# One decode step of attention with a gate: heads loaded whole into six slots, queries and gate made first, keys multiplied in place

## The chip, the cores and the metric

The kernel runs on one core of one Trainium2 chip. The core has a matrix engine (PE; its weight loads are shown apart as PEld), a vector engine (DVE), a scalar engine (ACT), GpSimd (POOL) and a queue engine (SP) that issues the loads; 16 transfer engines (DMA) carry them out. SBUF is the memory that the engines read, PSUM the one that PE writes. Lower is better: the metric is the device time in microseconds, the median of several runs. Instructions are named by their line in the kernel, as L204.

## The reference, cut to what matters

One token (`x`, 512 values) is normalised, attends to a cache of 8192 keys and values in each of 32 heads, and is multiplied by a gate. All is in float32.

```python
xn = layernorm(x)                                   # 512
q  = (xn @ wq).reshape(32, 128)                     # wq 512 x 4096
s  = einsum("hd,hkd->hk", q, k_cache) * 128**-0.5   # k_cache 32 x 8192 x 128
o  = einsum("hk,hkd->hd", softmax(s), v_cache)      # v_cache 32 x 8192 x 128
a  = o.reshape(4096) @ wo                           # wo 4096 x 512
g  = silu((sigmoid(xn @ w_gate) * (xn @ w_up)) @ w_down)   # 512 x 1376 twice, 1376 x 512
out = x + a * g
```

Keys and values are 268 MB, `wq` and `wo` 8.39 MB each, the gate's three weights 8.45 MB together. Each byte is used once.

## The kernel before

All loads go through SP's one queue, in the order in which the code asks for them, into ten slots of 16 KB per partition (`stream`). A load waits in the queue until its slot has no reader left. A head's 8192 cached rows lie as 64 rows on each of 128 partitions; a load brings 32 of the 64 (`CB`), so keys and values of a head are four loads of 2 MB. Head 0 and head 31 are cut smaller. Keys are asked for two heads ahead, values in the head itself. `wq` comes in four chunks of eight heads, `wo` in chunks of eight heads when these heads are done (the last ones in pieces), and the gate's weights in six pieces in heads 2 to 7.

The queries are needed on every partition. `queries(c)` (L130) makes them so at once: the normalised token is copied into 128 columns (`xnb`) and is the stationary operand, so that each partition of the result holds the same row `qb`.

For a head, DVE does the scores: `scores` (L199) takes 16 rows at a time, multiplies them by the query into a tile `prod` (L204; two buffers) and sums along the 128 values (L205), four times for a head. `row_max` (L207) takes the maximum on each partition and PE turns it into a row (`pt`, L211); `all_max` (L214) takes the maximum of that row on DVE (L215), PE spreads it (`pm`, L217), ACT scales it (L218) and makes the exponentials `pr` with their row sums `rs` (L221). `norm` (L230) adds the row sums over partitions on PE (`pl`, L232) and takes the reciprocal on DVE (`rl`, L234). `weighted` (L223) multiplies by the values: 64 matmuls of one column by 128, on four column tiles of PE that write partitions 0, 32, 64 and 96 (`po`, L226). A float32 matmul is two passes in the profile, so a head has 128 of them. `finish` (L236) turns the four partial rows into a column (`pT`, L240), and `project` (L244) multiplies it by `wo` into `acc` (L246).

The heads are a pipeline: in the pass for head h the scores of head h, the maximum of head h - 1 and the values of head h - 2 are written (`values(h - 2)`, L292). The order on each engine is then set by the framework's scheduler, which may move an instruction ahead of others. The gate is done in heads 9 and 11 (`glu_hidden` L165 with `pgu` L172 and `hid`, `glu_out` L179 with `pd` L185 and `g_row`).

Of the kernel before, what the change touches and what calls it, by code (L numbers as in the profile page):

```python
# [18 lines left out]
def kernel(  # L19
# [21 lines left out]
    FT = (F + P - 1) // P  # L41
    NG = 4                 # column tiles of the tensor engine
    GP = P // NG
    SCALE = float(Dh) ** -0.5
# [10 lines left out]
    slot_words = CB * Dh  # L55

    def slot(name, words):
        assert words <= slot_words
        return stream.tile([P, slot_words], F32, tag="stream", name=name)
# [3 lines left out]
    # rows of the output stand on the first partition of each column tile  # L63
    GC = D // NG
    x_row = const.tile([P, GC], F32, name="x_row")
    nc.vector.memset(x_row, 0.0)

    wq_t, wo_t, kv_t = {}, {}, {}

    def load_wq(c):  # L70
        t = slot(f"wq{c}", KT * HG * Dh).rearrange("p (k n) -> p k n", k=KT)
        nc.sync.dma_start(
            t, wq[:, c * HG * Dh:(c + 1) * HG * Dh].rearrange("(p k) n -> p k n", k=KT))
        wq_t[c] = t

    def load_rows(which, src, h, b0, n):
        t = slot(f"{which}{h}_{b0}", n * Dh)
        nc.sync.dma_start(
            t[:, :n * Dh],
            src[0, h, b0 * P:(b0 + n) * P, :].rearrange("(p j) d -> p (j d)", p=P))  # L80
        kv_t[which, h, b0] = t[:, :n * Dh].rearrange("p (j d) -> p j d", d=Dh)

    def load_wo(h0, n):
        t = slot(f"wo{h0}", n * D)[:, :n * D].rearrange("p (h e) -> p h e", e=D)
        nc.sync.dma_start(t, wo[h0 * Dh:(h0 + n) * Dh, :].rearrange("(h p) e -> p h e", p=Dh))
        for i in range(n):
            wo_t[h0 + i] = t[:, i, :]

    load_rows("k", k_cache, 0, 0, SB)
    nc.sync.dma_start(x_col, xv.rearrange("(p k) -> p k", k=KT))  # L90

# [7 lines left out]

    load_wq(0)  # L100
    for b in range(SB, NB, SB):
        load_rows("k", k_cache, 0, b, SB)
    nc.sync.dma_start(x_row[0:P:GP, :], xv.rearrange("(g c) -> g c", g=NG))

# [19 lines left out]
    xnb = const.tile([P, KT, P], F32, name="xnb")  # L124
    nc.vector.tensor_copy(xnb, xn.rearrange("p (k o) -> p k o", o=1).to_broadcast([P, KT, P]))

# [1 line left out]
    qb = const.tile([P, H * Dh], F32, name="qb")  # L128

    def queries(c):  # L130
        for n in range(HG * Dh // 512):
            pq = ps_big.tile([P, 512], F32, tag="ps_big", name=f"pq{c}_{n}")
            for k in range(KT):
                nc.tensor.matmul(pq, xnb[:, k, :], wq_t[c][:, k, n * 512:(n + 1) * 512],  # L134
                                 start=(k == 0), stop=(k == KT - 1))
            o0 = c * HG * Dh + n * 512
            nc.scalar.copy(qb[:, o0:o0 + 512], pq)  # L137

# [1 line left out]
    gl = {}  # L140

    def load_glu(step):
        hk = KT // 2
        if step < 4:
            name, src = (("wg", w_gate), ("wu", w_up))[step // 2]
            i = step % 2
            t = slot(f"{name}{i}", hk * F)[:, :hk * F].rearrange("p (k f) -> p k f", f=F)
            nc.sync.dma_start(t, src.rearrange("(p k) f -> p k f", k=KT)[:, i * hk:(i + 1) * hk, :])
            for k in range(hk):
                gl[name, i * hk + k] = t[:, k, :]  # L150
        else:
            f0, f1 = ((0, 6), (6, FT))[step - 4]
            t = slot(f"wd{f0}", (f1 - f0) * D)[:, :(f1 - f0) * D].rearrange("p (t e) -> p t e", e=D)
            full = min(f1, F // P)
            nc.sync.dma_start(t[:, :full - f0, :],
                              w_down[f0 * P:full * P, :].rearrange("(t p) e -> p t e", p=P))
            if full < f1:
                nc.sync.dma_start(t[:F - full * P, full - f0, :], w_down[full * P:F, :])
            for i in range(f0, f1):
                gl["wd", i] = t[:, i - f0, :]  # L160

    hid = const.tile([P, FT], F32, name="hid")
    g_row = const.tile([P, GC], F32, name="g_row")

    def glu_hidden():  # L165
        pgu = ps_big.tile([P, 512], F32, tag="ps_big", name="pgu")
        fl = F - (FT - 1) * P
        for a, name in enumerate(("wg", "wu")):
            for t in range(FT):
                m = min(P, F - t * P)  # L170
                for k in range(KT):
                    nc.tensor.matmul(pgu[:m, a * FT + t:a * FT + t + 1],  # L172
                                     gl[name, k][:, t * P:t * P + m], xn[:, k:k + 1],
                                     start=(k == 0), stop=(k == KT - 1))
        for rows, c0, c1 in ((P, 0, FT - 1), (fl, FT - 1, FT)):
            nc.scalar.activation(hid[:rows, c0:c1], pgu[:rows, c0:c1], AF.Sigmoid)  # L176
            nc.vector.tensor_mul(hid[:rows, c0:c1], hid[:rows, c0:c1], pgu[:rows, FT + c0:FT + c1])  # L177

    def glu_out():  # L179
        pd = ps_big.tile([P, 512], F32, tag="ps_big", name="pd")  # L180
        nc.vector.memset(pd[:, :GC], 0.0)
        for t in range(FT):
            m = min(P, F - t * P)
            for g in range(NG):
                nc.tensor.matmul(pd[g * GP:g * GP + 1, :GC], hid[:m, t:t + 1],  # L185
                                 gl["wd", t][:m, g * GC:(g + 1) * GC],
                                 start=(t == 0), stop=(t == FT - 1))
        nc.scalar.activation(g_row, pd[:, :GC], AF.Sigmoid)
        nc.vector.tensor_mul(g_row, g_row, pd[:, :GC])

# [6 lines left out]
    sc, mx, pr, rs, rl, oT = {}, {}, {}, {}, {}, {}  # L197

    def scores(h, b, n, i):  # L199
        if b + i == 0:  # L200
            sc[h] = work.tile([P, NB], F32, tag="sc", name=f"sc{h}")
        q = qb[:, h * Dh:(h + 1) * Dh].rearrange("p (o d) -> p o d", o=1).to_broadcast([P, n, Dh])
        prod = work.tile([P, SB, Dh], F32, tag="prod", name=f"prod{h}_{b + i}")
        nc.vector.tensor_mul(prod[:, :n, :], kv_t["k", h, b][:, i:i + n, :], q)  # L204
        nc.vector.reduce_sum(sc[h][:, b + i:b + i + n], prod[:, :n, :], axis=AX.X)  # L205
# [8 lines left out]
    def all_max(h, pt):  # L214
        nc.vector.reduce_max(mx[h][:1, 1:2], pt, axis=AX.X)  # L215
        pm = ps_s.tile([P, 1], F32, tag="ps_s", name=f"pm{h}")
        nc.tensor.matmul(pm, ones[:1, :], mx[h][:1, 1:2], start=True, stop=True)  # L217
        nc.scalar.mul(mx[h][:, 2:3], pm, -SCALE)  # L218
        pr[h] = work.tile([P, NB], F32, tag="pr", name=f"pr{h}", bufs=3)
        rs[h] = work.tile([P, 1], F32, tag="rs", name=f"rs{h}", bufs=3)  # L220
        nc.scalar.activation(pr[h], sc[h], AF.Exp, bias=mx[h][:, 2:3], scale=SCALE, accum_out=rs[h])  # L221

    def weighted(h, b0, n):  # L223
        for j in range(n):
            g = (b0 + j) % NG
            nc.tensor.matmul(po[h % 2][g * GP:g * GP + 1, :], pr[h][:, b0 + j:b0 + j + 1],  # L226
                             kv_t["v", h, b0][:, j, :],
                             start=(b0 + j < NG), stop=(b0 + j >= NB - NG))

    def norm(h):  # L230
        pl = ps_s.tile([P, 1], F32, tag="ps_s", name=f"pl{h}")
        nc.tensor.matmul(pl, ones, rs[h], start=True, stop=True)  # L232
        rl[h] = work.tile([P, 1], F32, tag="rl", name=f"rl{h}", bufs=3)
        nc.vector.reciprocal(rl[h], pl)  # L234

    def finish(h):  # L236
        o1 = work.tile([P, Dh], F32, tag="o1", name=f"o1_{h}")
        nc.scalar.copy(o1, po[h % 2])  # L238
        pT = ps_s.tile([P, 1], F32, tag="ps_s", name=f"pT{h}")
        nc.tensor.matmul(pT, o1, rl[h], start=True, stop=True)  # L240
        oT[h] = work.tile([P, 1], F32, tag="oT", name=f"oT{h}", bufs=HG + 2)
        nc.scalar.copy(oT[h], pT)

    def project(h):  # L244
        for g in range(NG):
# [106 lines left out]
```

## Time and profile before

| | |
|---|---|
| runs, median (lowest to highest) | 709.97 us (709.45 to 710.28), 3 runs |
| profiled execution, first to last instruction | 707.6 us |
| DVE busy | 586.9 us, 83% |
| PE busy / weight loads | 326.5 us, 46% / 223.7 us, 32% |
| ACT busy | 46.4 us, 7% |
| read from HBM | 293.67 MB, 415 GB/s over the span |
| transfer engines in use by SP's queue | 98.9% |
| granted TensorE clock, mean | 0.657 of full speed |

The profiled execution has no time of its own beside its span; the span is 2.4 us below the median of the runs. In a timeline's row stand the start (us), the time taken (us), engine, line and operation, the tiles (written<-read) with their shapes, how many instructions are merged in the row (x2), and in brackets how long the engine was idle before and what ended that. In a table of waits stand the engine and line that waited, what it waited for, and the sum in us, the times and the longest. In a table of windows stand the stretch, its length, busy time of PE, PEld, DVE, ACT and POOL, each with its count, the granted clock, the share of the transfer engines and GB/s.

### The profile page before, as it was taken

To read this page: it belongs to the slowest core of one execution; us is meant where nothing else is said; L and a number is where in the kernel's file an instruction comes from. 1 tells how busy PE (TensorE), PEld (TensorE's weight loads), DVE (VectorE), ACT (ScalarE), POOL (GpSimd) and SP (SyncE) were. 2 spreads that over 40 slices of the span, in tenths; PEclk is the share of its full clock that TensorE was granted. 3 is DMA by queue.
4 is the path that set the end of the run, shared out by engine and by line. 5 is a ranking of instruction groups with operands and counts; after the bars stand their busy time and mean duration, and the time that the engine had idled before them with its cause. 6 is when DMAs were issued, how large, how long until landed. Compare 5 with 4: busy or idle time off the path is not lost.

```text
span 707.6 us, 10924 instructions
## 1 busy us (share of the span) xinstructions
PE 326.5 (46%) x4940; PEld 223.7 (32%) x4940; DVE 586.9 (83%) x374; ACT 46.4 (7%) x178; POOL 0.7 (0%) x6
## 2 busy tenths in 40 slices
PE   3231444449974323444572244444463353334466
PEld 1021332228863222333251132223132232222244
DVE  1999988886058799888888898888888998888970
ACT  0010000000101101000000000000010000000000
POOL 0000000000000000000000000000000000000000
PEclk9655676667566665555586666655576676665558
DMA  8999999999999999999999999999999999999995
GB/s 349 432 423 427 425 430 425 421 427 370 400 421 400 428 427 426 427 423 424 428 429 412 430 426 425 426 428 423 427 427 428 414 427 428 429 426 423 425 416 239
DMA packets 28413, 294.36 MB, mean 416 GB/s; under 512 B 2664, under 2 KB 2672, under 8 KB 10704
## 3 DMA queue, kind: packets, MB, share of 16 engines
q1 hardware_dynamic: 28368, 293.68, 98.9%
q8 instruction: 38, 0.62, 0.4%
q14 instruction: 7, 0.06, 0.0%
HBM read 293.67 MB, written 0.00 MB: 415 GB/s over the span
## 4 chain that ended last, share of the span: by engine, by line
DVE 64%; issue 17%; PE 16%; DMA 3%; ACT 0%; SPq 0%
DVE prod L204 33%; DVE sc L205 28%; PE pgu L172 4%; PE pt L211 2%; PE pm L217 2%; PE pq L134 2%; PE pl L232 2%; PE po L226 2%; DMA wq<-in_A_wq_dram 1%; DMA wo<-in_A_wo_dram 1%; DVE mx L215 1%; DVE mx L209 1%; DVE rl L234 1%; PE pd L185 0%; ACT qb L137 0%
## 5 line engine op out<-in xcount | busy, mean ns | idle before, releaser
L204 DVE TENSOR_TENSOR prod<-k,qb 128x2048 f32<-128x2048 f32 x129 | 287.0, 2264 | 9.7 <-ACT qb L137 9.7
L205 DVE TENSOR_REDUCE sc<-prod 128x16 f32<-128x2048 f32 x129 | 286.5, 2261 | 0.0
L226 PE MATMUL po<-v,pr 128*1 128x128 f32 x4096 | 175.7, 347 | 52.2 <-DMA v<-in_A_v_cache_dram 50.2
L226 PEld LDWEIGHTS po<-v,pr 128*1 128x1 f32 x4096 | 121.1, 104 | 99.8 <-DMA v<-in_A_v_cache_dram 56.7
L211 PE MATMUL pt<-ident,mx 128*1 128x128 f32 x64 | 18.5, 391 | 274.8 <-DVE mx L209 274.8
L211 PEld LDWEIGHTS pt<-ident,mx 128*1 128x1 f32 x64 | 2.8, 81 | 278.4 <-DVE mx L209 258.4
L134 PE MATMUL pq<-wq,xnb 128*128 128x512 f32 x64 | 38.9, 775 | 3.8 <-DMA wq<-in_A_wq_dram 3.8
L234 DVE RECIPROCAL rl<-pl 128x1 f32<-128x1 f32 x32 | 5.3, 167 | 41.1 <-PE pl L232 41.1
L215 DVE TENSOR_REDUCE mx<-pt 1x1 f32<-1x128 f32 x32 | 8.9, 278 | 31.2 <-PE pt L211 31.2
L218 ACT ACTIVATE mx<-pm 128x1 f32<-128x1 f32 x32 | 5.5, 171 | 309.5 <-PE pm L217 309.5
L238 ACT COPY o<-po 128x128 f32<-128x128 f32 x32 | 8.5, 265 | 253.6 <-PE po L226 253.6
L217 PEld LDWEIGHTS pm<-mx,ones 1*128 1x128 f32 x64 | 15.7, 302 | 29.7 <-DVE mx L215 29.7
L217 PE MATMUL pm<-mx,ones 1*128 1x1 f32 x64 | 18.4, 354 | 14.0 <-DVE mx L215 13.9
L240 PE MATMUL pT<-rl,o 128*128 128x1 f32 x64 | 12.6, 266 | 25.5 <-DVE rl L234 14.6
L134 PEld LDWEIGHTS pq<-wq,xnb 128*128 128x128 f32 x64 | 15.9, 256 | 23.8 <-issue 23.8
L240 PEld LDWEIGHTS pT<-rl,o 128*128 128x128 f32 x64 | 9.9, 195 | 35.0 <-ACT o L238 20.1
L232 PE MATMUL pl<-rs,ones 128*128 128x1 f32 x64 | 18.4, 357 | 0.0
L172 PE MATMUL pgu<-xn,wu 128*128 128x1 f32 (+1 forms) x88 | 18.4, 345 | 0.0
L172 PEld LDWEIGHTS pgu<-xn,wu 128*128 128x128 f32 (+1 forms) x88 | 18.3, 325 | 0.0
L232 PEld LDWEIGHTS pl<-rs,ones 128*128 128x128 f32 x64 | 15.7, 306 | 0.7 <-issue 0.2
L177 DVE TENSOR_TENSOR hid<-hid,pgu 128x10 f32<-128x10 f32 (+1 forms) x2 | 0.3, 158 | 17.6 <-ACT hid L176 17.6
L172 PEld LDWEIGHTS pgu<-xn,wg 128*128 128x128 f32 (+1 forms) x88 | 13.5, 249 | 0.5 <-issue 0.5
(44 smaller groups left out, 91.8 us busy)
## 6 DMA issues: line engine op xcount, KB each, us to landing
k<-in_A_k_cache_dram SPq DMA_DIRECT2D x60, 2048.0 KB, 27.6
v<-in_A_v_cache_dram SPq DMA_DIRECT2D x60, 2048.0 KB, 25.8
wq<-in_A_wq_dram SPq DMA_DIRECT2D x4, 2048.0 KB, 21.9
k<-in_A_k_cache_dram SPq DMA_DIRECT2D x7, 1024.0 KB, 14.8
v<-in_A_v_cache_dram SPq DMA_DIRECT2D x7, 1024.0 KB, 23.4
wo<-in_A_wo_dram SPq DMA_DIRECT2D x3, 2048.0 KB, 22.8
wg<-in_B_w_gate_dram SPq DMA_DIRECT2D x2, 1376.0 KB, 26.8
wu<-in_B_w_up_dram SPq DMA_DIRECT2D x2, 1376.0 KB, 20.7
```

Of the source, the lines that this page charges most:

```text
L134: nc.tensor.matmul(pq, xnb[:, k, :], wq_t[c][:, k, n * 512:(n + 1) * 512], start=(k == 0), stop=(k == KT - 1))
L172: nc.tensor.matmul(pgu[:m, a * FT + t:a * FT + t + 1], gl[name, k][:, t * P:t * P + m], xn[:, k:k + 1], start=(k == 0), stop=(k == KT - 1))
L204: nc.vector.tensor_mul(prod[:, :n, :], kv_t["k", h, b][:, i:i + n, :], q)
L205: nc.vector.reduce_sum(sc[h][:, b + i:b + i + n], prod[:, :n, :], axis=AX.X)
L211: nc.tensor.matmul(pt, mx[h][:, 0:1], ident, start=True, stop=True)
L215: nc.vector.reduce_max(mx[h][:1, 1:2], pt, axis=AX.X)
L217: nc.tensor.matmul(pm, ones[:1, :], mx[h][:1, 1:2], start=True, stop=True)
L226: nc.tensor.matmul(po[h % 2][g * GP:g * GP + 1, :], pr[h][:, b0 + j:b0 + j + 1], kv_t["v", h, b0][:, j, :], start=(b0 + j < NG), stop=(b0 ...
L232: nc.tensor.matmul(pl, ones, rs[h], start=True, stop=True)
L234: nc.vector.reciprocal(rl[h], pl)
L238: nc.scalar.copy(o1, po[h % 2])
L240: nc.tensor.matmul(pT, o1, rl[h], start=True, stop=True)
```

## The change

Loads: ten slots of 16 KB become six of 32 KB per partition, and a load brings all 64 rows of a head's keys or values (4.19 MB). `wq` comes in two loads of half its rows, each gate weight in one load; they stand first in the queue, keys of head 0 behind them. `wo` comes last, in two halves (the second in three loads). Rows of `wo` and of `w_down` are dealt out to the partitions so that a partition's rows are neighbours in memory; for `w_down` this means that column t of a gate tile is every tenth column, and `wg` and `wu` are read with that step.

Queries: all 32 heads at once, as rows on partitions 0, 32, 64 and 96 (one column of `xn` is the stationary operand); `spread` (four heads at a time) multiplies such a row by ones to bring it to every partition. The gate follows at once. Scores: the product is written over the keys, and each product is followed by its own sum. Values: head h - 1 in the pass for head h, behind the first quarter of its scores, and `values` begins with `pl` and the reciprocal. The output columns are kept in `o_all`, and all projections follow the last head. `tc.manual_schedule()` keeps each engine's order as written.

```diff
-    CB = 32                # of those, rows in a load
-    HG = 8                 # heads in a chunk of wq or wo
+    SLOT = NB * Dh
+    ctx.enter_context(tc.manual_schedule())
-    stream = ctx.enter_context(tc.tile_pool(name="stream", bufs=10))
+    stream = ctx.enter_context(tc.tile_pool(name="stream", bufs=6))
...
+    nc.sync.dma_start(x_col, xv.rearrange("(p k) -> p k", k=KT))
+    load_wq(0)
+    nc.vector.memset(x_row, 0.0)
+    nc.sync.dma_start(x_row[0:P:GP, :], xv.rearrange("(g c) -> g c", g=NG))
+    load_wq(1)
+    load_gate("wg", w_gate)
+    load_gate("wu", w_up)
+    load_down()
...
+    for k in range(KT):
+        for b in range(NQ // NG):
+            for g in range(NG):
+                c = (b * NG + g) * QT
+                nc.tensor.matmul(pq[b][g * GP:g * GP + 1, :], xn[:, k:k + 1], wq_t[k][:, c:c + QT],
+                                 start=(k == 0), stop=(k == KT - 1))
+    for b in range(NQ // NG):
+        nc.scalar.copy(q_row[:, b, :], pq[b])
+    def spread(t):
+        b, g = divmod(t, NG)
+        pb = ps_big.tile([P, QT], F32, tag="ps_big", name=f"pb{t}")
+        nc.tensor.matmul(pb, ones[g * GP:g * GP + 1, :], q_row[g * GP:g * GP + 1, b, :],
+                         start=True, stop=True)
+        qb[t] = work.tile([P, QT], F32, tag="qb", name=f"qb{t}")
+        nc.scalar.copy(qb[t], pb)
+    spread(0)
...
+            cols = slice(t, FT * P, FT) if t < FT else slice(FT * P, F)
             for k in range(KT):
-                    nc.tensor.matmul(pgu[:m, a * FT + t:a * FT + t + 1],
-                                     gl[name, k][:, t * P:t * P + m], xn[:, k:k + 1],
+                nc.tensor.matmul(pgu[:m, a * NT + t:a * NT + t + 1], gl[name, k][:, cols], xn[:, k:k + 1],
                                  start=(k == 0), stop=(k == KT - 1))
...
-        prod = work.tile([P, SB, Dh], F32, tag="prod", name=f"prod{h}_{b + i}")
-        nc.vector.tensor_mul(prod[:, :n, :], kv_t["k", h, b][:, i:i + n, :], q)
-        nc.vector.reduce_sum(sc[h][:, b + i:b + i + n], prod[:, :n, :], axis=AX.X)
+        for j in range(j0, j1, SB):
+            kt = kv_t["k", h][:, j:j + SB, :]
+            nc.vector.tensor_mul(kt, kt, q)
+            nc.vector.reduce_sum(sc[h][:, j:j + SB], kt, axis=AX.X)
...
+        rows = slice(i * GP, (i + 1) * GP)
+        for r in range(R):
+            nc.tensor.matmul(pT[rows, r:r + 1], o1[:, r:Dh:R], rl[h], start=True, stop=True)
+        nc.scalar.copy(o_all[rows, w, :], pT[rows, :])
...
     for h in range(H):
-        for b, n in parts(h):
-            for i in range(0, n, SB):
-                scores(h, b, min(n, SB), i)
-                if b + i == 0 and h > 0:
-                    all_max(h - 1, pt)
-        if h > 1:
-            values(h - 2)
-        pt = row_max(h)
+        need(("k", h))
+        if h + 2 < H:
+            need(("k", h + 2))
+        if h % HT == HT - 2 and h + HT < H:
+            spread(h // HT + 1)
+        scores(h, 0, NB // 4)
+        if h > 0:
+            all_max(h - 1, pt)
+            need(("v", h - 1))
+            values(h - 1)
+        scores(h, NB // 4, NB)
+        pt = row_max(h)
+    need(order[-1])
+    all_max(H - 1, pt)
+    values(H - 1)
+    for w in range(NW):
+        project(w)
```

What this moves is seen in the rows of the engines' programs (line, operation, tile written<-tiles read; the number behind a name counts tiles). DVE, one head in the middle, before:

```order
L204 TENSOR_TENSOR prod_0_1475<-k_0_1174,qb 128x2048
L204 TENSOR_TENSOR prod_16_1485<-k_0_1174,qb 128x2048
L205 TENSOR_REDUCE sc_1474<-prod_0_1475 128x16
L205 TENSOR_REDUCE sc_1474<-prod_16_1485 128x16
L204 TENSOR_TENSOR prod_32_1488<-k_32_1176,qb 128x2048
L204 TENSOR_TENSOR prod_48_1491<-k_32_1176,qb 128x2048
L205 TENSOR_REDUCE sc_1474<-prod_32_1488 128x16
L205 TENSOR_REDUCE sc_1474<-prod_48_1491 128x16
L209 TENSOR_REDUCE mx_1568<-sc_1474 128x1
L215 TENSOR_REDUCE mx_1568<-pt_1570 1x1
L234 RECIPROCAL rl_1604<-pl_1602 128x1
```

DVE, one head in the middle, now (L213 is the product, L214 the sum, L218 the row maximum, L224 the maximum of the row `pt`, L236 the reciprocal):

```order
L213 TENSOR_TENSOR k_337<-k_337,qb_160 128x2048
L214 TENSOR_REDUCE sc_543<-k_337 128x16
L224 TENSOR_REDUCE mx_535<-pt_537 1x1
L236 RECIPROCAL rl_555<-pl_553 128x1
L213 TENSOR_TENSOR k_337<-k_337,qb_160 128x2048
L214 TENSOR_REDUCE sc_543<-k_337 128x16
L213 TENSOR_TENSOR k_337<-k_337,qb_160 128x2048
L214 TENSOR_REDUCE sc_543<-k_337 128x16
L213 TENSOR_TENSOR k_337<-k_337,qb_160 128x2048
L214 TENSOR_REDUCE sc_543<-k_337 128x16
L218 TENSOR_REDUCE mx_635<-sc_543 128x1
```

Products and sums alternate; the maximum of `pt` moved from the end of its own head into the next one, behind the first sum, and the reciprocal behind it now belongs to the same head as that maximum (before, to the head ahead of it).

DVE at the start, from the end of the normalisation to the first scores, before:

```order
L121 RECIPROCAL st<-st 128x1
L123 TENSOR_SCALAR xn<-xc,st 128x4
L125 COPY xnb<-xn 128x512
L204 TENSOR_TENSOR prod_0_156<-k_0_79,qb 128x2048
L204 TENSOR_TENSOR prod_16_159<-k_16_93,qb 128x2048
```

and now:

```order
L140 TENSOR_SCALAR xn<-xc,st 128x4
L147 MEMSET pq_120 128x512
L147 MEMSET pq_122 128x512
L184 TENSOR_TENSOR hid<-hid,pgu 128x10
L184 TENSOR_TENSOR hid<-hid,pgu 96x1
L186 MEMSET pd 128x128
L194 TENSOR_TENSOR g_row<-g_row,pd 128x128
L198 MEMSET acc 128x128
L201 MEMSET po_307 128x128
L201 MEMSET po_308 128x128
L213 TENSOR_TENSOR k_312<-k_312,qb_160 128x2048
```

The gate's two steps on DVE (`hid`, `g_row`) stand ahead of the first product. PE at the same place, before and then now:

```order
L134 MATMUL pq_0_127<-wq_91,xnb 128x512 x4
L134 MATMUL pq_1_133<-wq_91,xnb 128x512 x4
L211 MATMUL pt_170<-ident,mx_168 1x128
L217 MATMUL pm_185<-mx_168,ones 128x1
L226 MATMUL po_123<-v_0_147,pr_188 1x128 x16
```

```order
L153 MATMUL pq_122<-wq_85,xn 1x512 x4
L163 MATMUL pb_158<-q_row,ones 128x512
L180 MATMUL pgu<-xn,wg 128x1 x40
L180 MATMUL pgu<-xn,wg 96x1 x4
L180 MATMUL pgu<-xn,wu 128x1 x40
L180 MATMUL pgu<-xn,wu 96x1 x4
L190 MATMUL pd<-wd,hid 1x128 x44
L220 MATMUL pt_333<-ident,mx_331 1x128
L226 MATMUL pm_343<-mx_331,ones 128x1
L234 MATMUL pl_349<-rs_347,ones 128x1
L239 MATMUL po_307<-v_314,pr_346 1x128 x64
```

The gate's 88 and 44 matmuls moved from the tenth and twelfth head to the place between the queries and the first head's maximum, and `pl` of a head from two heads later to right behind its `pm`.

More of the change, by code (lines that the diff above doesn't have):

```diff
@@ L83, in load_wo, with load_wq @@
[L83 to L90, printed above, removed]
+    wq_t, kv_t, wo_t, gl = {}, {}, {}, {}
+    def load_wq(i):
+        n = KT // 2
+        t = slot(f"wq{i}").rearrange("p (k c) -> p k c", k=n)
+        nc.sync.dma_start(t, wq.rearrange("(p k) c -> p k c", k=KT)[:, i * n:(i + 1) * n, :])
+        for k in range(n):
+            wq_t[i * n + k] = t[:, k, :]
@@ new lines, in load_rows, with load_wo @@
+    def load_rows(which, src, h):
+        t = slot(f"{which}{h}")
+        nc.sync.dma_start(t, src[0, h].rearrange("(p j) d -> p (j d)", p=P))
+        kv_t[which, h] = t.rearrange("p (j d) -> p j d", d=Dh)
+    def load_wo(g0, n, cuts=()):
+        t = slot(f"wo{g0}").rearrange("p (g r e) -> p g r e", r=R, e=D)
+        src = wo[g0 * P * R:(g0 + n) * P * R, :].rearrange("(g p r) e -> p g r e", p=P, r=R)
+        m = n - 1 if cuts else n
+        nc.sync.dma_start(t[:, :m], src[:, :m])
+        for r0, r1 in cuts:
+            nc.sync.dma_start(t[:, m, r0:r1, :], src[:, m, r0:r1, :])
+        for i in range(n):
+            wo_t[g0 + i] = t[:, i]
@@ L123 @@
     nc.vector.tensor_scalar(xn, xc, st[:, 4:5], None, op0=ALU.mult)
[L124 to L132, printed above, removed]
+    q_row = const.tile([P, NQ // NG, QT], F32, name="q_row")
+    pq = []
+    for b in range(NQ // NG):
+        t = ps_big.tile([P, QT], F32, tag="ps_big", name=f"pq{b}")
+        nc.vector.memset(t, 0.0)
+        pq.append(t)
@@ L133, in queries @@
+    spread(0)
+    hid = const.tile([P, FT + 1], F32, name="hid")
+    g_row = const.tile([P, GC], F32, name="g_row")
+    pgu = ps_big.tile([P, 512], F32, tag="ps_big", name="pgu")
+    NT = FT + 1
+    for a, name in enumerate(("wg", "wu")):
+        for t in range(NT):
+            m = P if t < FT else FL
+            cols = slice(t, FT * P, FT) if t < FT else slice(FT * P, F)
             for k in range(KT):
-                nc.tensor.matmul(pq, xnb[:, k, :], wq_t[c][:, k, n * 512:(n + 1) * 512],
+                nc.tensor.matmul(pgu[:m, a * NT + t:a * NT + t + 1], gl[name, k][:, cols], xn[:, k:k + 1],
@@ L135, in queries @@
                                  start=(k == 0), stop=(k == KT - 1))
[L136 to L172, printed above, removed]
-                                     gl[name, k][:, t * P:t * P + m], xn[:, k:k + 1],
[L174 to L189, printed above, removed]
+    for rows, c0, c1 in ((P, 0, FT), (FL, FT, NT)):
+        nc.scalar.activation(hid[:rows, c0:c1], pgu[:rows, c0:c1], AF.Sigmoid)
+        nc.vector.tensor_mul(hid[:rows, c0:c1], hid[:rows, c0:c1], pgu[:rows, NT + c0:NT + c1])
@@ new lines @@
+    pd = ps_big.tile([P, 512], F32, tag="ps_big", name="pd")
+    nc.vector.memset(pd[:, :GC], 0.0)
+    for t in range(NT):
+        m = P if t < FT else FL
+        for g in range(NG):
+            nc.tensor.matmul(pd[g * GP:g * GP + 1, :GC], hid[:m, t:t + 1],
+                             gl["wd", t][:m, g * GC:(g + 1) * GC],
+                             start=(t == 0), stop=(t == NT - 1))
+    nc.scalar.activation(g_row, pd[:, :GC], AF.Sigmoid)
+    nc.vector.tensor_mul(g_row, g_row, pd[:, :GC])
@@ L218, in all_max @@
         nc.scalar.mul(mx[h][:, 2:3], pm, -SCALE)
-        pr[h] = work.tile([P, NB], F32, tag="pr", name=f"pr{h}", bufs=3)
-        rs[h] = work.tile([P, 1], F32, tag="rs", name=f"rs{h}", bufs=3)
+        pr[h] = work.tile([P, NB], F32, tag="pr", name=f"pr{h}")
+        rs[h] = work.tile([P, 1], F32, tag="rs", name=f"rs{h}")
         nc.scalar.activation(pr[h], sc[h], AF.Exp, bias=mx[h][:, 2:3], scale=SCALE, accum_out=rs[h])
[L223 to L228, printed above, removed]
@@ L230, in norm, with values @@
-    def norm(h):
+    def values(h):
         pl = ps_s.tile([P, 1], F32, tag="ps_s", name=f"pl{h}")
         nc.tensor.matmul(pl, ones, rs[h], start=True, stop=True)
-        rl[h] = work.tile([P, 1], F32, tag="rl", name=f"rl{h}", bufs=3)
+        rl[h] = work.tile([P, 1], F32, tag="rl", name=f"rl{h}")
         nc.vector.reciprocal(rl[h], pl)
-    def finish(h):
+        for j in range(NB):
+            g = j % NG
+            nc.tensor.matmul(po[h % 2][g * GP:g * GP + 1, :], pr[h][:, j:j + 1], kv_t["v", h][:, j, :],
+                             start=(j < NG), stop=(j >= NB - NG))
@@ L237, in finish @@
         o1 = work.tile([P, Dh], F32, tag="o1", name=f"o1_{h}")
         nc.scalar.copy(o1, po[h % 2])
[L239 to L245, printed above, removed]
-            nc.tensor.matmul(acc[g * GP:g * GP + 1, :], oT[h], wo_t[h][:, g * GC:(g + 1) * GC],
-                             start=(h == 0), stop=(h == H - 1))
@@ L270, with project @@
-    queries(0)
-    load_k(1)
+        w, i = divmod(h, R)
+        pT = ps_s.tile([P, R], F32, tag="ps_s", name=f"pT{h}")
+        rows = slice(i * GP, (i + 1) * GP)
+        for r in range(R):
+            nc.tensor.matmul(pT[rows, r:r + 1], o1[:, r:Dh:R], rl[h], start=True, stop=True)
+        nc.scalar.copy(o_all[rows, w, :], pT[rows, :])
+    def project(w):
+        for r in range(R):
+            for g in range(NG):
+                nc.tensor.matmul(acc[g * GP:g * GP + 1, :], o_all[:, w, r:r + 1],
+                                 wo_t[w][:, r, g * GC:(g + 1) * GC],
+                                 start=(w + r == 0), stop=(w == NW - 1 and r == R - 1))
@@ new lines, with issue, need @@
+    order = []
+    for h in range(H):
+        order.append(("k", h))
+        if h < H - 2:
+            order.append(("v", h))
+    order += [("v", H - 2), ("v", H - 1), ("wo", 0), ("wo", NW // 2)]
+    def issue(item):
+        which, i = item
+        if which == "wo":
+            load_wo(i, NW // 2, () if i == 0 else ((0, R - 1), (R - 1, R)))
+        else:
+            load_rows(which, k_cache if which == "k" else v_cache, i)
+    ahead = iter(order)
+    loaded = set()
+    def need(item):
+        while item not in loaded:
+            nxt = next(ahead)
+            issue(nxt)
+            loaded.add(nxt)
@@ L291 @@
-        if h > 1:
-            values(h - 2)
-        pt = row_max(h)
-        if (h + 2) % HG == 0 and h + 2 < H:
-            queries((h + 2) // HG)
-        if h == 9:
-            glu_hidden()
-        if h == 11:
-            glu_out()
-        if h > 2 and (h - 2) % HG == 0:
-            for i in range(h - 2 - HG, h - 2):
-                project(i)
-    for i in range(H - HG // 2, H):
-        load_wo(i, 1)
-    all_max(H - 1, pt)
-    values(H - 2)
-    for i in range(H - HG, H - HG // 2):
-        project(i)
@@ L311 @@
-    norm(H - 1)
-    for b, n in parts(H - 1):
-        weighted(H - 1, b, n)
-    for i in range(H - HG // 2, H - 2):
-        project(i)
-    finish(H - 1)
-    project(H - 2)
-    project(H - 1)
+            need(("k", h + 2))
[7 more added lines that the diff above has]
+        scores(h, NB // 4, NB)
+        pt = row_max(h)
```

80 lines of the change are left out of this document (29 added, 51 removed).

## The prediction

> **What bounds the kernel now.** I read the page's first and third parts, then the waits, then one head on the vector engine in order of time.
>
> ```profile
> span 707.6 us, 10924 instructions
> PE 326.5 (46%) x4940; PEld 223.7 (32%) x4940; DVE 586.9 (83%) x374; ACT 46.4 (7%) x178; POOL 0.7 (0%) x6
> q1 hardware_dynamic: 28368, 293.68, 98.9%
> ```
>
> Two resources are near full. The loads occupy the transfer engines for 98.9% of the span, and the vector engine (DVE) is busy for 83%. The waits tell which of them follows the other.
>
> ```profile
> SPq L78 <- DVE prod L204: 293.0, 48, 11.0
> DVE rl L234 <- PE pl L232: 41.1, 29, 8.1
> ```
>
> The load queue waits 293 us for DVE to free a slot. DVE never waits for keys; what it waits for is the small chain of the softmax (41.1 us for the sum behind `rl` alone). One head in the middle of the run:
>
> ```profile
> 303.69 0.22 DVE L209 TENSOR_REDUCE mx<-sc 128x1 f32<-128x64 f32 x1
> 304.58 0.28 DVE L215 TENSOR_REDUCE mx<-pt 1x1 f32<-1x128 f32 x1 [0.68 <-PE pt L211]
> 306.05 0.17 DVE L234 RECIPROCAL rl<-pl 128x1 f32<-128x1 f32 x1 [1.19 <-PE pl L232]
> 306.14 4.47 DVE L204 TENSOR_TENSOR prod<-k,qb 128x2048 f32<-128x2048 f32 x2
> 310.53 4.47 DVE L205 TENSOR_REDUCE sc<-prod 128x16 f32<-128x2048 f32 x2
> 314.92 4.49 DVE L204 TENSOR_TENSOR prod<-k,qb 128x2048 f32<-128x2048 f32 x2
> 319.31 4.47 DVE L205 TENSOR_REDUCE sc<-prod 128x16 f32<-128x2048 f32 x2
> 323.82 0.22 DVE L209 TENSOR_REDUCE mx<-sc 128x1 f32<-128x64 f32 x1
> ```
>
> From one row maximum to the next it is 20.13 us: four products and four sums, 17.6 us, and 2.5 us for the maximum, its two short waits and the reciprocal. A head's keys and values are 2 x 32768 x 128 bytes, 8.39 MB; at the 425 GB/s of a window below that is 19.7 us. So the two rates are nearly equal, DVE is a little the slower, and the load order lets the stream run ahead. Whatever lengthens DVE's head, or starts its first head later, therefore shows in the time almost in full.
>
> **The change, part by part.** First, the head on DVE. The products no longer go to two `prod` tiles, two products and then two sums, but in place: product, its own sum, next product. Two instructions that don't depend on each other start 2.20 us apart (306.14 to 310.53 for two), one alone lasts 4.47 - 2.20 = 2.27, and an instruction that reads its predecessor's result starts 0.04 after that one's end (319.31 + 4.47 to 323.82). A pair that depends costs 2.27 + 0.04 + 2.20 = 4.51 in place of 4.39. Four pairs: 18.04 us, 0.5 more than before. That the product overwrites its source I cost at nothing: the operand count and shape are as before. No row shows it; a row bound is 2.20 us for either kind of instruction, one element after the other, which leaves no gain.
>
> Second, the chain of a head's maximum, exponentials and sum. Before, the reciprocal behind head h - 1's maximum was that of head h - 2, whose row sums were long there; it waited only for the matrix engine (PE) to come round. Now it is head h - 1's own, so DVE stands still for the whole chain from the maximum to the sum. The links, in order of time, from the second last head:
>
> ```profile
> 667.13 0.28 DVE L215 TENSOR_REDUCE mx<-pt 1x1 f32<-1x128 f32 x1 [0.68 <-PE pt L211]
> 667.47 0.58 PE L217 MATMUL pm<-mx,ones 1*128 1x1 f32 x2 [0.37 <-DVE mx L215]
> 667.98 0.59 PE L232 MATMUL pl<-rs,ones 128*128 128x1 f32 x2
> 668.09 0.17 ACT L218 ACTIVATE mx<-pm 128x1 f32<-128x1 f32 x1 [4.73 <-PE pm L217]
> 668.29 0.35 ACT L221 ACTIVATE pr<-sc,mx 128x64 f32<-128x64 f32 x1
> 668.54 0.19 ACT L221 ACTIVATION_READ_ACCUMULATOR pr<-sc,mx 128x1 f32 x1
> ```
>
> From the maximum's end (667.41) to the row sums (668.73) it is 1.32 us; `pl` then needs 0.05 + 0.59 + 0.04. That is a wait of 2.00 us, where 1.19 stood. Against it, the wait of 0.68 for `pt` goes: a product and a sum, 4.5 us, now lie between the row maximum and its use. The head after the change is 18.04 + 0.28 + 2.00 + 0.09 (reciprocal, less the overlap with the next product) + 0.26 (last sum's end and row maximum) = 20.67 us, 0.54 more than before. Behind the waiting reciprocal stand the six large instructions left of the head; nothing else runs on DVE meanwhile. Head 0 has no such chain: 18.3. All heads: 18.3 + 31 x 20.67 = 659.1 us. The first exponentials also load their table, 1.28 us by a row below, now inside the wait: 1.3 once.
>
> Third, the start, where most of the time goes. Before, 1 MB of keys and 2 MB of `wq` came first and DVE began the first head at 19.06 us. Now all of `wq` (8.39 MB) and of the gate's weights (8.45 MB) stand ahead of the first keys, and the written order keeps the gate's last product ahead of the first head on DVE. Rates of the loads at the start, and what PE does for the queries and the copies after them:
>
> ```profile
> 2.00:14.00 12.00, 3.24 (x7) 2.07 (x8) 1.69 (x8) 0.28 (x2) 0.00 (x0) 1.00 0.98 376
> 14.00:20.00 6.00, 6.00 (x11) 2.45 (x11) 0.94 (x1) 0.58 (x1) 0.00 (x0) 1.00 1.04 440
> 20.00:40.00 20.00, 2.43 (x7) 0.65 (x5) 20.00 (x11) 0.58 (x1) 0.00 (x0) 0.61 1.00 425
> 153.32 9.20 PE L134 MATMUL pq<-wq,xnb 128*128 128x512 f32 x16
> 18.45 0.58 ACT L137 COPY qb<-pq 128x512 f32<-128x512 f32 x1 [10.03 <-PE pq L134]
> ```
>
> The last column is GB/s: 4.51 MB by 14 us, 7.15 by 20, then 425. `wq` is complete at 22.9 us, 23.3 with the issue of `x_col` ahead of it. By the same rate the gate's three weights are in at 29.9, 36.5 and 43.1, and the first keys at 53.1. The query matmuls stand on one row of each column tile, as those of `po` do. Their second half is 32 passes of 512 columns; `po`'s 128-column passes take 0.051 us (6.49 / 128, row in the tail) or 0.030 (1.93 / 64), so 6.5 or 3.9 us; I take the middle, 5.2, to 28.5. Two copies of 0.58 with their gaps, 1.2, to 29.7; the spread of the first query is two passes at 9.20 / 16, 1.2, to 30.9. Then PE does the gate:
>
> ```profile
> 162.36 13.41 PE L172 MATMUL pgu<-xn,wg 128*128 128x1 f32 x88
> 175.63 0.99 PE L172 MATMUL pgu<-xn,wu 128*128 128x1 f32 x4
> 184.59 17.42 PE L172 MATMUL pgu<-xn,wu 128*128 128x1 f32 x84
> 163.00:168.00 5.00, 5.00 (x46) 5.00 (x45) 5.00 (x3) 0.14 (x1) 0.00 (x0) 0.98 1.02 434
> 190.00:196.00 6.00, 6.00 (x30) 6.00 (x29) 0.00 (x0) 0.00 (x0) 0.00 (x0) 0.50 1.05 438
> 202.04 0.18 ACT L176 ACTIVATE hid<-pgu 128x10 f32<-128x10 f32 x1 [15.65 <-PE pgu L172]
> 202.66 0.15 DVE L177 TENSOR_TENSOR hid<-hid,pgu 96x1 f32<-96x1 f32 x1 [0.23 <-ACT hid L176]
> 242.82 2.09 PE L185 MATMUL pd<-wd,hid 128*1 128x128 f32 x35
> 243.07 1.28 ACT L188 ACT_TABLE_LOAD   x1
> 245.50 0.29 DVE L189 TENSOR_TENSOR g_row<-g_row,pd 128x128 f32<-128x128 f32 x1 [2.40 <-ACT g_row L188]
> ```
>
> The first 176 passes took 31.8 us before, 0.109 us each at a granted clock of 0.98 and 0.200 at 0.50 (46 in 5 us, 30 in 6). They were spread over other work's time; now they lie on the path: from 30.9 to 62.7. The bounds are 176 x 0.109 = 19.2 and 176 x 0.200 = 35.2; I keep 31.8, since queries run ahead of the gate in both kernels. The hidden row's sigmoid and product, 0.8 (202.04 to 202.81), to 63.5; its 88 passes at 2.09 / 35, 5.3, to 68.8; the last sigmoid, product and three memsets, 1.1, to 69.9. So DVE starts the first head at 69.9 us, 16.8 after its keys are there. In front of it nothing else hides this: DVE has no other work.
>
> One more price lies in the gate. `wg` and `wu` are now read by every tenth column (a step of 40 bytes), where 128 neighbours were read. No row has such a read; the bounds are no change and, by the nearest row, twice the 31.8 us if each weight costs as much as two. I take no change, as the slow passes at clock 0.50 leave 1.6 ns for each weight. [...]
>
> Fourth, the tail, with the rows of before:
>
> ```profile
> 687.61 6.49 PE L226 MATMUL po<-v,pr 128*1 128x128 f32 x128
> 694.49 0.38 PE L240 MATMUL pT<-rl,o 128*128 128x1 f32 x2
> 695.88 1.93 PE L226 MATMUL po<-v,pr 128*1 128x128 f32 x64
> 704.45 0.29 DVE L321 TENSOR_TENSOR res<-g_row,acc 128x128 f32<-128x128 f32 x1 [8.29 <-PE acc L246]
> 705.09 0.60 SPq L323 DMA_DIRECT2D out_dram<-res  x1
> ```
>
> After the last row maximum come `pt` and the maximum (0.96), the chain (2.0), 128 passes of `po` (6.4), the copy (0.4), four `pT` pairs (1.2; four rows of 0.38 are the upper bound), a copy (0.3), and then all 256 projection passes, which before ran in four groups beside the heads. At 0.030 they take 7.7 us, at 0.051 13.1; I take 7.7, as PE has been busy since `po`. The end from 704.40 on is 3.2. Sum: 22.1 us, as much as before (685.57 to 707.6), so the projections' move eats what the late `wo` loads cost.
>
> Fifth, the stream. Pieces of 32 KB per partition and six slots hold 25 MB. A key slot comes free at its head's end, so its next keys are asked for two heads, 41 us, ahead and need 9.9 us plus at most one load in front. The loads are hidden; if that cover goes, each late piece costs DVE its lateness. That `wo` stands last costs nothing: its slots come free two heads before the end.
>
> The sum: 69.9 + 659.1 + 1.3 + 22.1 = 752.4 us of span. The profiled execution of before has 707.6 and the median of the runs is 710.0; with the same 2.4 us around it, 755 us.
>
> **The rivals.** *Weights by columns read at half speed.* For it: the step of 40 bytes, untested here. Against it: the passes are slow already. The start goes to 101.7, the time to 787. *The gate at the full clock.* For it: the windows from 2 to 20 us grant 1.00, and the query passes just ahead keep PE busy. Against it: in the same situation before, the clock fell to 0.50 within 10 us. The gate then takes 19.2 and the time is 742. *Faster: the stream sets the pace.* If the wait of 2.00 us vanished, a head would take 18.7, less than the loads' 19.7, and the time would be what 293.68 MB at 425 GB/s need, 691 us, with 2 at the start, 10 behind the last piece and the 2.4 around: 705. For it: 98.9% in the queue's row. Against it: the written order puts the reciprocal before three quarters of the head, with its own chain. It decides only where the wait falls below some 0.5 us: (710 - 2.4 - 69.9 - 18.3 - 1.3 - 22.1) / 31 = 19.2 us a head. *The loads come late.* If the large pieces ran at 390 GB/s for want of requests, a head would need 21.5 us and the time would be about 780. Against it: from the second head on two loads are waiting.
>
> **How the numbers follow.** The likeliest, a late start and a head of 20.7, has 0.62, with its own range from 748 to 762. Half-speed weights 0.17, the full clock 0.13, late loads 0.04, the stream 0.03, and 0.01 that gains and losses cancel. 0.2% is about what a measurement of this kernel can tell from no change. Slower are all but the last two, 0.96; faster 0.03, same 0.01. The range from 742 to 788 takes in the second and third case.
>
> **What would show it.** In the profile after: the first product on DVE near 70 us, behind `g_row`; the reciprocal's wait at 2.0 us each, 62 us in all; none of `mx` for `pt`; head after head 20.7 us apart; the loads' share near 93% and some load waits ended by DVE; 256 passes of `acc` in one piece at the end. I am wrong if the first product comes before 60 or after 80 us, if the heads lie under 20 us apart, or if DVE waits for keys.

## The result, and the profile after

| | median (lowest to highest) | profiled span |
|---|---|---|
| before | 709.71 us (708.85 to 710.28), 4 runs | 707.6 us |
| changed | 760.44 us (759.25 to 760.72), 4 runs | 758.9 us |

The changed kernel takes 1.071 times as long (95% interval 1.070 to 1.073): 51 us slower. The forecast was 755, in a range from 742 to 788. One of the four runs of the first experiment below, the profiled one, fell in a slower state of the chip and took 737.2 us, so its time there is the median of the other three, 699.9 us (700.2 with all four), and its profile is not used.

First the parts of the page of the changed kernel that answer to those shown of before.

```profile
span 758.9 us, 11178 instructions
PE 334.6 (44%) x5148; PEld 232.9 (31%) x5148; DVE 596.6 (79%) x373; ACT 43.6 (6%) x177; POOL 0.7 (0%) x6
q1 hardware_dynamic: 11424, 293.68, 92.6%
```

The same 293.68 MB in fewer packets, but the transfer engines are now idle for 7% of the span. The waits say for whom, of DVE and of the load queue:

```profile
DVE rl L236 <- PE pl L234: 64.9, 32, 3.3
DVE hid L184 <- ACT hid L183: 62.7, 2, 62.4
SPq L92 <- PE po L239: 356.0, 29, 13.1
SPq L92 <- DVE mx L218: 240.2, 29, 19.0
```

The queue waits for slots that DVE (keys) and PE behind DVE (values) free; DVE waits for keys in no row. Its own two large waits are the reciprocal's, 64.9 us in 32 heads, and the one ahead of the first head. One head of the changed kernel on DVE:

```profile
406.12 0.22 DVE L218 TENSOR_REDUCE mx<-sc 128x1 f32<-128x64 f32 x1
406.26 2.28 DVE L213 TENSOR_TENSOR k<-k,qb 128x2048 f32<-128x2048 f32 x1
408.64 2.29 DVE L214 TENSOR_REDUCE sc<-k 128x16 f32<-128x2048 f32 x1
410.85 0.27 DVE L224 TENSOR_REDUCE mx<-pt 1x1 f32<-1x128 f32 x1
413.10 0.17 DVE L236 RECIPROCAL rl<-pl 128x1 f32<-128x1 f32 x1 [1.99 <-PE pl L234]
413.19 2.27 DVE L213 TENSOR_TENSOR k<-k,qb 128x2048 f32<-128x2048 f32 x1
415.50 2.29 DVE L214 TENSOR_REDUCE sc<-k 128x16 f32<-128x2048 f32 x1
417.70 2.28 DVE L213 TENSOR_TENSOR k<-k,qb 128x2048 f32<-128x2048 f32 x1
...
426.86 0.22 DVE L218 TENSOR_REDUCE mx<-sc 128x1 f32<-128x64 f32 x1
```

From row maximum to row maximum it is 20.74 us. The maximum of `pt` no longer waits; the reciprocal behind it waits 1.99. The product over the keys takes 2.28, as the product into `prod` did.

The start, from the timelines of PE and DVE and a table of windows:

```profile
29.98 19.47 PE L180 MATMUL pgu<-xn,wg 128*128 128x1 f32 x88 [0.34 <-DMA wg<-in_B_w_gate_dram]
49.31 19.46 PE L180 MATMUL pgu<-xn,wu 128*128 128x1 f32 x88
69.86 4.79 PE L190 MATMUL pd<-wd,hid 128*1 128x128 f32 x88 [1.09 <-ACT hid L183]
75.04 0.29 DVE L194 TENSOR_TENSOR g_row<-g_row,pd 128x128 f32<-128x128 f32 x1 [5.28 <-ACT g_row L193]
75.70 2.27 DVE L213 TENSOR_TENSOR k<-k,qb 128x2048 f32<-128x2048 f32 x1
40.00:50.00 10.00, 10.00 (x49) 10.00 (x48) 0.00 (x0) 0.00 (x0) 0.00 (x0) 0.50 1.05 430
```

PE works on the gate from 29.98 to 68.8 us without a gap, most of it at a granted clock of 0.50. Then come `hid`, `pd` and `g_row`, and only then, at 75.70, the first product. The end, with the last row maximum of before (line L209) ahead of it:

```profile
685.35 0.22 DVE L209 TENSOR_REDUCE mx<-sc 128x1 f32<-128x64 f32 x1
```

```profile
737.91 0.22 DVE L218 TENSOR_REDUCE mx<-sc 128x1 f32<-128x64 f32 x1
740.97 6.53 PE L239 MATMUL po<-v,pr 128*1 128x128 f32 x128
747.89 0.46 PE L247 MATMUL pT<-rl,o 128*32 128x1 f32 x5 [0.40 <-ACT o L242]
748.38 7.17 PE L253 MATMUL acc<-wo,o_all 128*1 128x128 f32 x250
755.58 0.29 DVE L302 TENSOR_TENSOR res<-g_row,acc 128x128 f32<-128x128 f32 x1 [14.33 <-PE acc L253]
```

So the 51.3 us between the two profiled spans divide as follows. Before, DVE's first product was at 19.06 us.

| stretch | before | changed | difference |
|---|---|---|---|
| start to the first product on DVE | 19.06 | 75.70 | +56.6 |
| first product to the end of the last row maximum | 666.5 | 662.4 | -4.1 |
| from there to the end | 22.0 | 20.8 | -1.2 |

The middle is shorter, though a head takes 0.6 us longer, because before it also held the gate. DVE stood still for it three times, in all 32 us: 12.2 for `pt`, which came behind the gate's first passes on PE (the other waits of that row are 0.68 each), 17.6 for `hid` and 2.4 for `g_row`:

```profile
DVE mx L215 <- PE pt L211: 31.2, 29, 12.2
DVE hid L177 <- ACT hid L176: 17.6, 2, 17.3
DVE g_row L189 <- ACT g_row L188: 2.4, 1, 2.4
```

In return, DVE did its first four heads without a wait, in 9 us less than four later ones.

### The profile page after: what moved, and what is told of

Read it like the earlier page. It is cut to its first block, busy times and chain, and to the rows that moved or that the text cites. A ratio compares the mean times of both kernels' runs of the same rounds, so it can differ in the third digit from the quotient of the medians.

```text
span 758.9 us, 11178 instructions
## 1 busy us (share of the span) xinstructions
PE 334.6 (44%) x5148; PEld 232.9 (31%) x5148; DVE 596.6 (79%) x373; ACT 43.6 (6%) x177; POOL 0.7 (0%) x6
## 3 DMA queue, kind: packets, MB, share of 16 engines
q1 hardware_dynamic: 11424, 293.68, 92.6%
## 4 chain that ended last, share of the span: by engine, by line
DVE 78%; PE 13%; DMA 4%; ACT 3%; issue 2%; SPq 0%; DVEq 0%
DVE sc L214 39%; DVE k L213 37%; PE pgu L180 5%; DMA wg<-in_B_w_gate_dram 4%; PE pl L234 3%; PE pm L226 3%; ACT pr L230 2%; PE acc L253 1%; PE po L239 1%; DVE mx L218 1%; DVE mx L224 1%; ACT mx L227 1%; DVE rl L236 1%; PE pd L190 1%; ACT L230 0%
## 5 line engine op out<-in xcount | busy, mean ns | idle before, releaser
L214 DVE TENSOR_REDUCE sc<-k 128x16 f32<-128x2048 f32 x128 | 292.6, 2286 | 6.5
L213 DVE TENSOR_TENSOR k<-k,qb 128x2048 f32<-128x2048 f32 x128 | 291.8, 2280 | 0.0
L239 PE MATMUL po<-v,pr 128*1 128x128 f32 x4096 | 183.3, 362 | 0.0
L239 PEld LDWEIGHTS po<-v,pr 128*1 128x1 f32 x4096 | 126.0, 109 | 48.4
L236 DVE RECIPROCAL rl<-pl 128x1 f32<-128x1 f32 x32 | 5.4, 168 | 64.9 <-PE pl L234 64.9
L247 PE MATMUL pT<-rl,o 128*32 128x1 f32 x256 | 20.5, 201 | 12.6 <-ACT o L242 12.6
L247 PEld LDWEIGHTS pT<-rl,o 128*32 128x32 f32 x256 | 17.8, 154 | 22.0 <-ACT o L242 22.0
L180 PEld LDWEIGHTS pgu<-xn,wg 128*128 128x128 f32 (+1 forms) x88 | 19.4, 316 | 1.1 <-ACT q_row L156 1.1
L180 PE MATMUL pgu<-xn,wg 128*128 128x1 f32 (+1 forms) x88 | 19.5, 358 | 0.3 <-DMA wg<-in_B_w_gate_dram 0.3
L153 PE MATMUL pq<-wq,xn 128*1 128x512 f32 x64 | 10.1, 790 | 13.8 <-DMA wq<-in_A_wq_dram 13.8
L163 PE MATMUL pb<-q_row,ones 1*128 1x512 f32 x16 | 15.6, 1074 | 0.0
```

The costliest lines, as they stand in the source:

```text
L163: nc.tensor.matmul(pb, ones[g * GP:g * GP + 1, :], q_row[g * GP:g * GP + 1, b, :], start=True, stop=True)
L180: nc.tensor.matmul(pgu[:m, a * NT + t:a * NT + t + 1], gl[name, k][:, cols], xn[:, k:k + 1], start=(k == 0), stop=(k == KT - 1))
L213: nc.vector.tensor_mul(kt, kt, q)
L214: nc.vector.reduce_sum(sc[h][:, j:j + SB], kt, axis=AX.X)
L239: nc.tensor.matmul(po[h % 2][g * GP:g * GP + 1, :], pr[h][:, j:j + 1], kv_t["v", h][:, j, :], start=(j < NG), stop=(j >= NB - NG))
L247: nc.tensor.matmul(pT[rows, r:r + 1], o1[:, r:Dh:R], rl[h], start=True, stop=True)
```

## The experiments

All are edits of the changed kernel; before was measured beside them at 710.0 us.

**The reciprocal behind the scores.** The wait for `pl` is taken away by giving it something to stand behind.

```diff
             values(h - 1)          # without its reciprocal and pT
         scores(h, NB // 4, NB)
+        if h > 0:
+            columns(h - 1, *part)  # reciprocal, pT, copy to o_all
         pt = row_max(h)
```

> Edit: the reciprocal of head h-1 (and the transposing matmuls that read it) is written behind the last score sum of head h, where its sum has long been ready; nothing else moves. Theory A (DVE's own order is the pace: the wait of 1.99 us per head is paid in full): the wait goes in all 31 heads, a head takes 18.7 us, the time falls by about 60 us to 698 to 702, below the kernel before, and DVE begins to wait for keys near the end. Theory B (the loads are the pace, 405 GB/s in the middle because pieces are large and few are asked for): a head stays at 20.7 us, DVE waits for keys instead, 755 to 760.

Measured: 699.9 us, 0.985 of before (0.983 to 0.988). One edit brings 60 us back and turns a loss of 7% into a gain of 1.5%. Theory A holds: DVE's order was the pace of the changed kernel, the stream was not. That the wait goes is seen in the trace of the kernel with two edits further on, which keeps this one: one wait of the reciprocal is left, 2.0 us.

**Three products, then three sums.**

```diff
-            nc.vector.tensor_mul(kt, kt, q)
-            nc.vector.reduce_sum(sc[h][:, j:j + SB], kt, axis=AX.X)
+            for j in js[a:a + 3]: ... tensor_mul(kt, kt, q)
+            for j in js[a:a + 3]: ... reduce_sum(sc[h][:, j:j + SB], kt, axis=AX.X)
```

> Edit: of a head's last three pieces, three products are written first and then three sums; still in place. Theory A: three dependent neighbours fewer per head, 0.12 us each, 0.36 us per head: a head of 20.4 us, 749 us. Rival (the order of products and sums costs nothing, the longer head comes from the chain alone): 760 us, no change.

Measured: 747.5 us, 12.9 less than the changed kernel. Two successive heads on DVE of this kernel:

```profile
406.72 0.17 DVE L240 RECIPROCAL rl<-pl 128x1 f32<-128x1 f32 x1 [1.99 <-PE pl L238]
406.81 6.67 DVE L215 TENSOR_TENSOR k<-k,qb 128x2048 f32<-128x2048 f32 x3
413.40 6.66 DVE L218 TENSOR_REDUCE sc<-k 128x16 f32<-128x2048 f32 x3
...
427.08 0.17 DVE L240 RECIPROCAL rl<-pl 128x1 f32<-128x1 f32 x1 [1.99 <-PE pl L238]
```

Three start-to-start steps take 6.59 us, 2.20 each, and a head 20.36, 0.38 less; 32 heads make 12.2 of the 12.9. The rival, that this order costs nothing, falls.

**Loads in halves.**

```diff
-        nc.sync.dma_start(t, rows)
+        nc.sync.dma_start(t[:, :SLOT // 2], rows[:, :SLOT // 2])
+        nc.sync.dma_start(t[:, SLOT // 2:], rows[:, SLOT // 2:])
```

> Edit: each load of keys or values is cut into two loads of 16 KB per partition into the same slot. Theory A: the load's size plays no part, since the loads follow DVE: 760 us, within 0.3%, GB/s in the middle still near 405. Theory B (large pieces lower the rate): the rate rises towards 425 and the time falls by up to 4%.

Measured: 759.2 us, against 760.4. The window from 140 to 640 us has the rate at which DVE takes the rows, as in the changed kernel (second fence, the same window):

```profile
140.00:640.00 500.00, 206.40 (x3428) 137.94 (x3432) 444.44 (x267) 28.86 (x129) 0.00 (x0) 0.63 0.98 406
```

```profile
140.00:640.00 500.00, 207.84 (x3422) 138.30 (x3422) 445.64 (x266) 28.41 (x127) 0.00 (x0) 0.62 0.97 406
```

The size of a load plays no part that this shows. That the stream can do more than 406 GB/s with pieces of 4.19 MB is seen in the last experiment, where it ran at 432 from 300 to 500 us.

**Gate weights as neighbours.**

```diff
-            cols = slice(t, FT * P, FT) if t < FT else slice(FT * P, F)
+            cols = slice(t * P, (t + 1) * P) if t < FT else slice(FT * P, F)
-        ... w_down[:FT * P, :].rearrange("(p t) e -> p t e", t=FT)
+        ... w_down[:FT * P, :].rearrange("(t p) e -> p t e", p=P)
```

> Edit: w_down's rows are dealt out as in the kernel before, so that the gate's weights are read as 128 neighbours instead of every tenth column. Theory A1 (the step costs little: 0.221 us a pass against 0.200 at the same clock of 0.50): the gate takes 32 to 35 us instead of 38.9, the first product on DVE comes at 69 to 72 us, the time is 754 to 757. Theory A2 (the step costs nothing, the low clock and the lack of other work make the 38.9): 760 us. Theory A3 (the step doubles a pass): cannot be more than half of 38.9, the time would fall by 19 us to 741.

Measured: 755.7 us (754.1 to 757.8). The gate's passes of this kernel:

```profile
29.83 15.85 PE L180 MATMUL pgu<-xn,wg 128*128 128x1 f32 x88 [0.67 <-ACT qb L166]
45.54 18.48 PE L180 MATMUL pgu<-xn,wu 128*128 128x1 f32 x88
```

They take 34.2 us in place of 38.8: the step costs 4.6 us. The time falls by 4.7, though so close an agreement is luck: the four runs lie 3.7 us apart, and the profiled span falls by 6.1, of which 1.4 are the last head's `po` (see the projections below). Of the 4.6 us, 3.6 are in `wg`, whose first passes meet the higher clock, and 1.0 in `wu`, all at 0.50. The windows from 30 to 32 us, of the changed kernel and then of this one, show why:

```profile
30.00:32.00 2.00, 2.00 (x10) 2.00 (x10) 0.00 (x0) 1.55 (x2) 0.00 (x0) 1.00 0.89 385
30.00:32.00 2.00, 2.00 (x20) 2.00 (x19) 0.00 (x0) 1.08 (x1) 0.00 (x0) 1.00 0.92 396
```

At a granted clock of 1.00, 10 passes with the step run in 2 us, against 20 of neighbours. At 0.50, in `wu`, it is 0.221 us a pass (19.46 / 88) against 0.210 (18.48 / 88). So in these two traces the step doubled a pass where the clock was 1.00 and cost 5% where it was 0.50. A1 holds for the gate as a whole; A3, a doubling of all its passes, is excluded.

**The gate's last steps behind the first heads.** The loads and the 176 passes stay; `hid` and `pd` follow the scores of head 0, the last sigmoid and `g_row` head 1.

```diff
         scores(h, NB // 4, NB)
+        if h == 0:
+            pd = gate_hidden()
         pt = row_max(h)
+        if h == 1:
+            gate_out(pd)
```

> Edit: only DVE's, ACT's and PE's steps behind the gate's first 176 passes move: hid and pd behind the scores of head 0, the last sigmoid and g_row behind head 1. The loads' order and the passes stay. Theory A (the late start is paid in full because the first product stands behind g_row in DVE's order): the first product comes when the keys are in, near 53 us instead of 75.7, the time falls by 20 to 22 us to 738 to 740. Rival (the start is hidden later, since the loads must be waited for anyway): under 5 us.

Measured: 740.3 us, 20.1 less. DVE's first product here:

```profile
54.32 2.29 DVE L198 TENSOR_TENSOR k<-k,qb 128x2048 f32<-128x2048 f32 x1 [47.33 <-DMA k<-in_A_k_cache_dram]
```

It comes when the keys are in, at 54.3. So of the 56.6 us by which the start was later, 21.4 are the place of `g_row` in DVE's order. The other 35 stood ahead as loads (and the 1 MB first piece of before against 4 MB); no run here loads keys ahead of the weights, so that part is read from the two traces, not tried.

**Projections ahead of the last head.**

```diff
+        if h == H - 1:
+            need(order[-1])
+            for w in range(NW - 1):
+                project(w)
         pt = row_max(h)
...
-    for w in range(NW):
-        project(w)
+    project(NW - 1)
```

> Edit: the projections of the first seven groups of four heads are written behind the values of head 30, where PE idles while DVE does the last scores, and only the last group at the end. Theory A (the 256 passes at the end lie on the path): 224 passes of 0.028 us, 6.3 us less at most, 754 to 757. Rival (the end is set by something else): 760.

Measured: 752.9 us, 7.6 less, more than the 6.3 that the passes weigh. The last head of this kernel has the rest:

```profile
739.76 0.46 PE L234 MATMUL pl<-rs,ones 128*128 128x1 f32 x2 [0.73 <-ACT pr L230]
740.15 5.21 PE L239 MATMUL po<-v,pr 128*1 128x128 f32 x128
```

The 128 passes of `po` take 5.21 us in place of 6.53. That PE comes from the projections and not from a pause does not explain it: in the kernel with gate weights as neighbours PE comes to the last head from a pause of 8.1 us, and its `po` is as short:

```profile
733.50 0.58 PE L220 MATMUL pt<-ident,mx 128*1 128x128 f32 x2 [8.07 <-DVE mx L218]
736.29 5.11 PE L239 MATMUL po<-v,pr 128*1 128x128 f32 x128
```

So 6.3 us belong to the edit, and the other 1.3 need not. In the traces of the changed kernel and of its edits, the last `po` takes between 5.11 and 6.53 us, and of three of them it is the shorter, the higher the clock granted over it: 6.53 us at 0.55 in the changed kernel, 5.21 at 0.69 here, 5.11 at 0.71 with neighbours. What sets that clock, no run here shows.

**Two edits, and three.** With the late reciprocal DVE no longer decides, so what does?

> Edit: the late reciprocal and the three products in a row, with the gate ahead of the first head as in the changed kernel. It tells what bounds the run with the late reciprocal alone (700.2 us): if DVE, 11 us less, about 689 to 691; if the stream, no change, 698 to 701.

> Edit: the late reciprocal, the three products in a row and the gate's steps behind head 0, together (projections at the end, as their weights are the last load). Theory A: DVE's work would end near 645 us, so the stream is the pace at last: 293.68 MB at 425 to 430 GB/s, 685 to 691 us, then one group's projection and the output, 693 to 700 us. If the loads cannot stay ahead with six slots, it is over 705.

Measured: 699.5 us (0.985 of before, 0.984 to 0.986) with two edits and 699.6 with the gate's steps moved as well, against 699.9 with the late reciprocal alone. What saved 12.9 and 20.1 us where DVE was the pace now saves 0.4 us and nothing. Of the kernel with two edits, DVE's waits and windows:

```profile
DVE k L215 <- DMA k<-in_A_k_cache_dram: 17.8, 15, 2.4
DVE rl L249 <- PE pl L238: 2.0, 1, 2.0
```

```profile
300.00:500.00 200.00, 90.36 (x1556) 61.62 (x1556) 190.96 (x115) 12.34 (x54) 0.00 (x0) 0.63 1.00 432
640.00:690.00 50.00, 26.72 (x544) 19.63 (x547) 36.81 (x24) 3.25 (x16) 0.00 (x0) 0.65 0.91 387
```

DVE waits for keys, and the stream runs at 432 GB/s with no idle share. It is the pace. In both kernels the last head's `po` starts at 680.2 us, and the tail behind the last keys has the same parts: their scores, the chain, `po` and 7.2 us of projections, which stand where nothing hides them.

## Why the prediction was right, point by point

| term | forecast | measured |
|---|---|---|
| end of the query matmuls | 28.5 | 28.6 |
| gate's 176 passes | 31.8 | 38.8 |
| first product on DVE | 69.9 | 75.7 |
| first keys in | 53.1 | 54.3 (gate's steps moved) |
| wait of the reciprocal, per head | 2.00 | 1.99 |
| head on DVE | 20.67 | 20.74 |
| all heads, with the table's load | 660.4 | 662.4 |
| tail | 22.1 | 20.8 |
| around the span | 2.4 | 1.5 |
| time | 755 | 760.4 |

The mechanism held in each part: the reciprocal's chain paid in full and 60 us of the time with it, the dependent product and sum, the first head behind `g_row`, the stream not the pace.

The mis-sized term is the gate. I kept the 31.8 us of before with the step of 40 bytes costed at no change; it took 38.8, 7.0 more. The experiment with neighbours puts 4.6 of it on the step. The remaining 2.4 (34.2 against 31.8) are all in `wg`, 15.85 us against 13.41. I put them on fewer passes at the higher clock: in before it was 1.00 from 162 to 166 us and 0.94 to 168, in the experiment 1.00 from 30 to 32 and 0.68 to 34. That was not tried by itself. Even my upper bound, 176 passes at 0.200, was passed: it was a bound for reads of neighbours, and a little low for them too (0.210 in `wu`). The traces speak against the step: with it 10 passes ran in 2 us, against 20, at the clock of 1.00, and a pass of `wu` took 0.221 us, against 0.210, at 0.50. My rival of twice the time was an estimate that no row of before showed. It did not come for the sum (38.8 us with the step, 34.2 with neighbours), since most passes ran at 0.50. The reason that I gave, that slow passes leave time for each weight, was an estimate too; it fits this, and no run tests it by itself. Where the clock was 1.00, the doubling did come.

One reading of mine was wrong, without harm to the sum: the gate's passes of before were not just spread over other work's time. DVE stood still for 32 us for the gate. So the change moved that cost to the start; it did not put it on the path for the first time.

Ahead of the gate and behind it the start took 1.2 us less than forecast. The other terms nearly cancel, by chance: heads +2.0 (the sum behind the first product of a head starts 0.10 behind it, not 0.04: 408.64 against 406.26 + 2.28), tail -1.3 (the four `pT` pairs and the last copy run beside the first projections), around the span -0.9.

Of the rivals, the gate at the full clock failed: 0.50 was granted for most of it, and the full clock would not have given its 19.2 us, since passes with the step took 0.20 us there too. Late loads failed: DVE never waited for keys. The stream as the pace was right in its condition: as soon as the wait was gone, the time was 699.9, where I had worked out 705.

## What to carry to other kernels

In DVE's written order a reciprocal of 0.17 us that waited for a chain over three engines cost the chain in each head, 1.99 us; written behind the next long piece of work, it waited once in the run with two edits, for 2.0 us. Look for such a short instruction ahead of long ones, and move it behind them. A busy share does not tell which of two nearly full resources is the pace; ask which of them waits for the other, and expect a gain on the one to end where the other takes over (here 60 us from the first edit, and 0.4 from the next two). Work that is put ahead of the first long loop is on the path from the moment at which the loop's first data are there: here 21.4 us of it, behind the 54.3 that the loads took.

## What the runs showed of the hardware that was not expected

PE was never idle from 29.98 to 68.8 us, and in that time the granted clock fell: 1.00 to 32 us, 0.87 from 32 to 34, 0.50 from there on. These were passes of one column, each behind a load of 128 columns. The 256 projection passes at the end ran at 1.00 from 748.4 to 755.5 us, at 0.028 us each. What in the two kinds of work decides the clock, no run here shows.

Reading float32 weights with a step of 40 bytes doubled a pass at the granted clock of 1.00 (10 in 2 us, against 20) and cost 5% at 0.50 (0.221 us, against 0.210). Here the price of a read pattern at one clock did not tell that at the other.
